# Tanh results in a four-buffer pool, three attention pairs begun a step earlier, weight sums begun later

## The chip, the core and the metric

The kernel runs on one NeuronCore of a Trainium2 chip. The metric is the device time of one execution in microseconds (us). Engines are named as in the profile: PE is TensorE's matmul, PEld its weight load, DVE is VectorE, ACT is ScalarE, POOL is GpSimd, and SP issues the transfers.

## The reference

Masked attention for 8 batches and 8 heads (576 rows, head size 64): the first four heads see a local band of 32 keys, the other four see every 32nd key. Its output, 4608 tokens of 512, goes through a two-layer network with a gate.

```python
scores = scale * np.matmul(q, k.transpose(0, 1, 3, 2))
scores = np.where(masks[None, :, :, :], scores, -1000000000.0)
scores = scores - np.max(scores, axis=-1, keepdims=True)
attn = np.exp(scores)
attn = attn / (np.sum(attn, axis=-1, keepdims=True) + 1e-09)
...
h = x @ w_in
g = h * (1.0 / (1.0 + np.exp(-1.702 * h)))
return (g @ w_out).astype(np.float32)
```

## The kernel before, in words

**Tiles and stages.** Tokens are cut into 9 groups of 512 (`NG`), the hidden width of 2048 into 16 blocks of 128 (`NF`). Each fp32 matrix is held as a high and a low part (`gh`, `gl`; `w_0` is the tile of both parts of an input weight block, `w_1` of an output weight block), and a product is three matmuls. The first three groups (`NN`) go through 48 **steps** `s`, one for each group and block: `ffn1(s)` makes `h` (12 matmuls), `act(s)` makes tanh on ACT and the gate on DVE, `split(s)`, at the following step, makes `gh` on ACT and `gl` on DVE, and `second` multiplies block s-2 into four output banks `o` (12 matmuls). The other six groups go in three doubles through a scheme with fewer products, which needs sums of weight blocks. That part begins at about 333 us and is not edited.

**Weights.** In the first 16 steps the weights are also unpacked. For each of two items a step, ACT shifts the raw words (`raw`), DVE joins them (`join`), ACT copies the high part (`high`), and DVE subtracts the low part (`low`). The weight block that is finished in step s is read by `ffn1(s+1)`.

**Attention in pairs.** Attention is done in pairs of head groups beside the steps. Pairs 0 to 4 come first. Pairs 5 to 9 are `apart`, the first group: they are turned in steps 5, 7, 9, 11 and 13 (`TURNS`). At step `begin[p]` a pair has its scores (PE: `s`), mask and maximum (DVE). Between `begin[p]` and `turn[p]` ACT makes its eight exponentials, spread over the steps between; what is left is run at step `turn[p]`, ahead of `high`. Then come a reciprocal (DVE), a multiply by it (POOL: `pr<-pr,rinv`), the transposes (DVE: `pt_s`, `pt_l`), and two steps after the turn the product with V (PE: `sa`), which ACT copies and DVE subtracts into `xs` or `xl`.

**Sums.** For each of 8 pairs of weight blocks `add_up(c)` runs six adds on POOL at the end of step `SUMS[c]`; two steps later ACT makes the high part (`plain<-summed`), three steps later DVE the low part, and SP stores eight pieces (`s<-plain`, `s<-summed`). The tiles come from one pool of 42 buffers shared with weights and attention results, so `summed` of block pair 1 takes the buffer that `plain` of block pair 0 left, and POOL waits until its stores have landed.

**Order.** Every engine keeps the order in which the program is written. No planner changes it; pools choose buffers. One pool of four buffers (`st2`) holds the output tiles of groups 0 and 1 until their stores have landed, one word tile, and, later, results of the doubles. The banks `c` of pairs 10 and later share six PSUM banks with `h` and `o`.

Of the kernel before, what the change touches and what calls it, by code (L numbers as in the profile page):

```python
# [9 lines left out]
F32 = mybir.dt.float32  # L10
# [8 lines left out]
P = 128  # L19
# [21 lines left out]
G = 512  # L41
# [12 lines left out]
AHEAD = 2  # L54
# [6 lines left out]
TURNS = ((5, 7, 9, 11, 13), (1, 3, 5, 7, 9, 11, 13, 15), (1, 3, 5, 7, 9, 11, 13))  # L61
BLOCKS = ("a11", "s2", "a12", "s3", "a22", "s1", "s4")
OPENING = ("a11", "a12", "s1", "s2", "s3", "a22", "s4")
SUMS = (17,19,21,29,31,33,35,37)
CUTS = (256, 384, 512)
PLAN = {
# [38 lines left out]
def attn_ffn(ctx, tc, lqk, sqk, lv, sv, w_in, w_out, masks, out):  # L105
# [7 lines left out]
    ffn = ctx.enter_context(tc.tile_pool(name="ffn", bufs=2))  # L113
# [7 lines left out]
    def st2(shape, dtype, name):  # L121
        return st.tile(shape, dtype, tag="st2", name=name, bufs=NT)
# [228 lines left out]
    apart = range(n0, n0 + len(windows[0]))  # L351
# [188 lines left out]
    g2s = {}  # L540

    def act(s):
        ps = hps.pop(s)
        g2 = g2s[s] = ffn.tile([P, G], F32, tag="g2", name=f"g2_{s}", bufs=1)
        scalar.activation(g2, ps, AF.Tanh, scale=0.851)
        vector.scalar_tensor_tensor(
            out=g2, in0=g2, scalar=1.0, in1=ps, op0=ALU.add, op1=ALU.mult
        )
# [137 lines left out]
    for p in (n0, n0 + 1):  # L686
        load_qk(p)
        load_v(p)
    act(0)
    weigh(3)  # L690
    split(0)
    begin_word(5)
    act(1)

    turn = {}
    p = n0
# [6 lines left out]
        turn[p + i] = len(steps) + 2 + 2 * i  # L703
    begin = {p: turn[p] - 3 for p in turn}
    for p in turn:
        if p - AHEAD in turn:
            begin[p] = turn[p - AHEAD] + (3 if p - AHEAD in apart else 2)

    sums = [
# [36 lines left out]
    def sum_up(s, end):  # L746
        for c in range(NF // 2):
            at = s - SUMS[c]
            if at == 0 and end:
# [234 lines left out]
    for s in range(2, len(steps)):  # L984
# [17 lines left out]
        for k in now:  # L1002
            low(k)
        act(s)
        ahead(s, False)
        sum_up(s, False)
# [28 lines left out]
    p = plain[-1] + 1  # L1035
# [8 lines left out]
    for d, (a, b) in enumerate(DOUBLES):  # L1044
# [20 lines left out]
        p = more.stop  # L1065
# [127 lines left out]
```

## Time and profile before

| | |
|---|---|
| median of 3 runs | 866.83 us (866.13 to 870.11) |
| profiled execution | 866.99 us, span 865.2 us, granted clock 0.99 |
| PE busy | 848.6 us, 98% |
| PEld busy | 689.6 us, 80% |
| DVE, ACT, POOL busy | 557.9, 439.6, 198.7 us |

Matmuls overlap in the profile, so that PE appears busy nearly always; how densely it is fed shows in PEld, the weight loads, one for each matmul. Every helper records its operations on one line of the source, L142, so tiles and not lines tell operations apart. Below, a step is named by when its `h` begins: step 9 at 77.71 us, step 10 at 85.67, step 15 at 126.09.

### The profile page before, as it was taken

How to read it: one execution, taken by the hardware profiler on the slowest of the kernel's cores; microseconds unless marked ns; L12 is line 12 of the kernel's file. 1: busy time of each engine (PE TensorE's matmuls, PEld its weight loads, DVE VectorE, ACT ScalarE, POOL GpSimd, SP SyncE). 2: the span in 40 equal slices, each digit the busy share in tenths (PEclk: the TensorE clock that was granted, in tenths of full speed). 3: DMA queues.
4: the chain of work that ended last, by engine and by line, in shares of the span. 5: the costliest groups of instructions: out<-in, count | busy, mean ns of one | idle time of the engine just before them, and what ended most of it. 6: DMA issues, size and time to landing. Idle time of an engine off the chain costs nothing.

```text
span 865.2 us, 17304 instructions
## 1 busy us (share of the span) xinstructions
PE 848.6 (98%) x6538; PEld 689.6 (80%) x6538; DVE 557.9 (64%) x989; ACT 439.6 (51%) x1330; POOL 198.7 (23%) x177
## 2 busy tenths in 40 slices
PE   8999989999999999999999999999999999999998
PEld 5887768877888888888888788888888888888886
DVE  4788977566587777766767776766766554444522
ACT  7798776453465555545545654545534433332321
POOL 4001003421366100423332011232230012232200
PEclk9899999999999999999999999999999999999999
DMA  9774324675165416666667645656655255454432
GB/s 341 298 283 152 121 62 145 203 229 175 47 225 167 153 47 207 195 204 214 182 192 233 191 135 162 219 172 196 182 165 177 72 164 166 151 169 142 149 119 74
DMA packets 76164, 148.87 MB, mean 172 GB/s; under 512 B 8240, under 2 KB 22960, under 8 KB 76080
## 3 DMA queue, kind: packets, MB, share of 16 engines
q1 hardware_dynamic: 76080, 147.76, 53.3%
q8 instruction: 52, 0.85, 0.4%
q14 instruction: 32, 0.26, 0.1%
HBM read 111.03 MB, written 36.70 MB: 171 GB/s over the span
## 4 chain that ended last, share of the span: by engine, by line
PE 88%; DVE 4%; ACT 3%; DMA 2%; SPq 1%; issue 1%; POOL 0%; ACTq 0%; DVEq 0%; POOLq 0%
PE o L142 42%; PE hs L142 15%; PE h L142 13%; PE ha L142 11%; PE sa L142 3%; PE c L142 2%; ACT pr L142 2%; SPq L142 1%; DMA s<-plain 1%; DVE w L142 1%; PE t L142 1%; DVE pt_l L142 1%; DMA a<-w 1%; PE s L142 1%; PE a L142 1%
## 5 line engine op out<-in xcount | busy, mean ns | idle before, releaser
L142 PE MATMUL o<-w,gh 128*128 128x512 f32 x1152 | 379.7, 391 | 0.1
L142 PEld LDWEIGHTS o<-w,gh 128*128 128x128 f32 x1152 | 216.5, 188 | 44.8 <-ACT out L142 0.6
L142 PE MATMUL o<-w,gl 128*128 128x512 f32 x576 | 228.3, 396 | 0.0
L142 POOL TENSOR_TENSOR gl<-y,gh 128x512 fp32r<-128x512 f32 x45 | 61.7, 1372 | 293.1 <-PE ha L142 149.8
L142 PEld LDWEIGHTS o<-w,gl 128*128 128x128 f32 x576 | 108.3, 188 | 24.3 <-DVE gl L142 0.2
L142 POOL TENSOR_TENSOR pr<-pr,rinv 128x432 f32<-128x432 f32 (+1 forms) x42 | 48.9, 1164 | 244.1 <-DVE rinv L142 244.1
L142 DVE SCALAR_TENSOR_TENSOR y<-tanh,y 128x512 f32<-128x512 f32 x96 | 67.8, 707 | 55.6 <-ACT tanh L142 55.5
L142 ACT ACTIVATE pr<-pr,nmax 128x54 f32<-128x54 f32 (+1 forms) x296 | 101.0, 344 | 4.9 <-DVE nmax L142 4.9
L142 ACT ACTIVATE tanh<-y 128x512 f32<-128x512 f32 x96 | 60.7, 632 | 67.5 <-DVE y L142 66.9
L142 PE MATMUL h<-xl,w 128*128 128x512 f32 x288 | 77.0, 403 | 5.6 <-ACT w L142 3.3
L142 PE MATMUL h<-xs,w 128*128 128x512 f32 x288 | 75.2, 397 | 0.0
L142 DVE TENSOR_TENSOR spare<-hs,spare 128x512 f32<-128x512 f32 x69 | 47.7, 691 | 38.9 <-PE hs L142 38.9
L142 DVE TENSOR_TENSOR gl<-spare,gh 128x512 fp32r<-128x512 f32 x48 | 33.2, 691 | 56.3 <-ACT gh L142 56.1
L142 PEld LDWEIGHTS h<-xl,w 128*128 128x128 f32 x288 | 54.0, 192 | 18.8 <-ACT w L142 3.7
L142 PEld LDWEIGHTS h<-xs,w 128*128 128x128 f32 x288 | 55.5, 193 | 11.9
L142 ACT CAST gh<-spare 128x512 fp32r<-128x512 f32 x48 | 29.9, 623 | 63.8 <-PE o L142 62.4
L142 DVE STREAM_TRANSPOSE pt_l<-pr 32x256 f32<-32x256 f32 x128 | 55.7, 435 | 5.8 <-POOL pr L142 3.7
L142 ACT ACTIVATE g<-h 128x512 f32<-128x512 f32 x48 | 28.7, 597 | 60.4 <-DVE gl L142 32.8
L142 DVE STREAM_TRANSPOSE pt_s<-pr 32x256 f32<-32x256 f32 x126 | 54.8, 435 | 3.1 <-POOL pr L142 1.1
L142 ACT ACTIVATION_READ_ACCUMULATOR pr<-pr,nmax 128x1 f32 x296 | 55.7, 188 | 0.0
L142 DVE SCALAR_TENSOR_TENSOR g<-g,h 128x512 f32<-128x512 f32 x48 | 32.9, 685 | 30.8 <-ACT g L142 30.8
L142 ACT COPY spare<-ha 128x512 f32<-128x512 f32 x24 | 14.1, 586 | 72.3 <-PE ha L142 72.3
(131 smaller groups left out, 1249.5 us busy)
## 6 DMA issues: line engine op xcount, KB each, us to landing
stream<-s SPq DMA_DIRECT2D x96, 256.0 KB, 2.7
stream<-a SPq DMA_DIRECT2D x72, 256.0 KB, 2.8
gate<-y SPq DMA_DIRECT2D x48, 256.0 KB, 2.6
spare<-gate SPq DMA_DIRECT2D x48, 256.0 KB, 2.8
qk<-sqk SPq DMA_DIRECT2D x23, 452.0 KB, 3.5
qk<-lqk SPq DMA_DIRECT2D x18, 576.0 KB, 3.9
v<-lv SPq DMA_DIRECT2D x18, 512.0 KB, 5.5
out<-out SPq DMA_DIRECT2D x36, 256.0 KB, 2.8
```

The lines of the kernel that those rows point to most:

```text
L142: ins = call(*args, **kw)
```

## The change

Three edits. The tanh of the 48 steps writes into a tile of the four-buffer pool `st2` and no longer into a single buffer `g2`. Pairs 7, 8 and 9 begin three steps ahead of their turn (at 6, 8 and 10) and no longer one step ahead (8, 10 and 12). The sums of block pair 1 move from step 19 to step 21, those of block pair 2 from 21 to 29, and each later one moves two steps, the last from 37 to 39.

```diff
-SUMS = (17,19,21,29,31,33,35,37)
+SUMS = (17, 21, 29, 31, 33, 35, 37, 39)
...
     def act(s):
         ps = hps.pop(s)
-        g2 = g2s[s] = ffn.tile([P, G], F32, tag="g2", name=f"g2_{s}", bufs=1)
+        g2 = g2s[s] = st2([P, G], F32, f"g2_{s}")
         scalar.activation(g2, ps, AF.Tanh, scale=0.851)
...
     for p in turn:
-        if p - AHEAD in turn:
+        if p - AHEAD in turn and p not in apart:
             begin[p] = turn[p - AHEAD] + (3 if p - AHEAD in apart else 2)
```

On ACT, from the end of step 8 into step 9, the order differs as follows. `gh` is the high part of the gate, `pr_98` the exponentials of pair 7, `w_0` and `w_1` the high parts of the weights of which the next `h` reads the first, `g_9` the tanh.

```order
-L142 CAST gh_1124<-g_8_1062 128x512
-L142 ACTIVATE pr_98,ssum_1128<-pr_98,nmax_1105 128x54 x8
-L142 ACTIVATE rinv_1137<-ssum_1128 128x8
-L142 CAST w_0_1141<-raw_860 128x512
-L142 CAST w_1_1143<-raw_863 128x512
-L142 ACTIVATE g_9_1151<-h_1109 128x512
+L142 ACTIVATE pr_98,ssum_1015<-pr_98,nmax_967 128x54 x4
+L142 CAST gh_1157<-g_8_1091 128x512
+L142 ACTIVATE rinv_1161<-ssum_1015 128x8
+L142 CAST w_0_1165<-raw_860 128x512
+L142 CAST w_1_1167<-raw_863 128x512
+L142 ACTIVATE g_9_1175<-h_1142 128x512
```

Eight exponentials stood between `gh` and the weights' high parts; now the last four stand ahead of `gh`, at the end of step 8, and nothing long stands ahead of the weights. The first four have moved to the end of step 7, where ACT's order in the changed kernel is this (`xs_0` are the copies of pair 5's product with V):

```order
L142 ACTIVATE raw_783<-raw_783 128x512 x2
L142 ACTIVATE pr_98,ssum_1015<-pr_98,nmax_967 128x54 x4
L142 CAST xs_0_311<-sa_5_1032 128x2x14x6
L142 CAST xs_0_311<-sa_5_1033 128x2x14x6
L142 CAST xs_0_1050<-sa_5_1032 128x2x4x6
L142 CAST xs_0_1050<-sa_5_1033 128x2x4x6
L142 CAST gh_1077<-g_7_1004 128x512
```

The copies that stood right behind `raw` now come four exponentials later. Steps 9 to 13 change in the same way for pairs 8 and 9.

On POOL, before, from the end of step 19 (`plain`, `summed` are tiles of the sums, `pr_97` and `pr_98` the scaled exponentials of pairs 12 and 13):

```order
L142 TENSOR_TENSOR plain_1961<-w_0_514 128x512
L142 TENSOR_TENSOR plain_1961<-w_0_646 128x512
L142 TENSOR_TENSOR summed_1962<-plain_1961 128x256 x2
L142 TENSOR_TENSOR summed_1962<-summed_1962,plain_1961 128x256
L142 TENSOR_TENSOR summed_1962<-plain_1961,summed_1962 128x256
L142 TENSOR_TENSOR pr_97<-pr_97,rinv_2045 128x8x54
L142 TENSOR_TENSOR plain_2118<-w_0_722 128x512
L142 TENSOR_TENSOR plain_2118<-w_0_775 128x512
L142 TENSOR_TENSOR summed_2119<-plain_2118 128x256 x2
```

In the changed kernel the same place reads:

```order
L142 TENSOR_TENSOR pr_97<-pr_97,rinv_2037 128x8x54
L142 TENSOR_TENSOR plain_2109<-w_0_514 128x512
L142 TENSOR_TENSOR plain_2109<-w_0_646 128x512
L142 TENSOR_TENSOR summed_2110<-plain_2109 128x256 x2
L142 TENSOR_TENSOR summed_2110<-summed_2110,plain_2109 128x256
L142 TENSOR_TENSOR summed_2110<-plain_2109,summed_2110 128x256
L142 TENSOR_TENSOR pr_98<-pr_98,rinv_2184 128x768
L142 TENSOR_TENSOR pr_97<-pr_97,rinv_2335 128x768
```

The multiply of pair 12 now precedes the sums of block pair 1, and the multiply of pair 13 no longer has the sums of block pair 2 ahead of it.

## Rows read from the trace of the kernel before

**Rows 1.** The page: busy time, share of the span and instructions of each engine.

```profile
PE   848.6 (98%) x6538; PEld 689.6 (80%) x6538; DVE 557.9 (64%) x989; ACT 439.6 (51%) x1330; POOL 198.7 (23%) x177
```

**Rows 2.** Busy time by stretches of 40 us; last three: PEclk, DMA share, GB/s.

```profile
80.00:120.00 40.00, 34.43 (x340) 26.23 (x339) 33.00 (x63) 29.92 (x93) 3.29 (x3) 0.94 0.37 120
...
160.00:200.00 40.00, 36.77 (x356) 29.62 (x355) 26.52 (x50) 18.67 (x75) 12.00 (x13) 0.96 0.76 243
...
240.00:280.00 40.00, 40.00 (x409) 32.64 (x408) 31.34 (x54) 22.44 (x79) 25.65 (x26) 1.00 0.61 193
```

**Rows 3.** Same view: steps 3 to 8, then steps 9 to 14.

```profile
42.30:77.71 35.41, 35.41 (x247) 28.62 (x241) 32.27 (x59) 33.16 (x88) 2.91 (x2) 1.00 0.59 216
...
77.71:126.09 48.38, 42.81 (x406) 32.83 (x400) 40.59 (x77) 36.52 (x107) 3.29 (x3) 0.93 0.33 106
```

**Rows 4.** PE in order of time: start, us, what, [idle before and its releaser].

```profile
85.67 0.73 PE L142 MATMUL h<-xl,w 128*128 128x512 f32 x2 [1.16 <-ACT w L142]
...
102.94 1.20 PE L142 MATMUL h<-xl,w 128*128 128x512 f32 x4 [1.11 <-DVE w L142]
...
117.72 0.80 PE L142 MATMUL h<-xl,w 128*128 128x512 f32 x2 [2.14 <-ACT w L142]
```

**Rows 5.** The chain that ended last, at step 9.

```profile
82.14 2.71 ACT pr L142 x16
```

**Rows 6.** Waits of DVE, 65.8 to 129.3 us: total us, times, longest.

```profile
DVE rinv L142 <- ACT rinv L142: 4.1, 3, 1.5
DVE w L142 <- ACT w L142: 3.2, 6, 0.7
```

**Rows 7.** DVE in order of time: the pairs of low parts of weights.

```profile
69.64 2.52 DVE L142 TENSOR_TENSOR w<-raw,w 128x512 fp32r<-128x512 f32 x2
...
85.65 1.87 DVE L142 TENSOR_TENSOR w<-raw,w 128x512 fp32r<-128x512 f32 x2 [0.33 <-ACT w L142]
...
91.87 1.28 DVE L142 TENSOR_TENSOR w<-raw,w 128x512 fp32r<-128x512 f32 x2
...
101.08 2.41 DVE L142 TENSOR_TENSOR w<-raw,w 128x512 fp32r<-128x512 f32 x2 [0.35 <-ACT w L142]
```

**Rows 8.** POOL in order of time, steps 21 to 24.

```profile
167.48 1.43 POOL L142 TENSOR_TENSOR summed<-plain 128x256 f32<-128x256 f32 x2 [12.81 <-DMA s<-plain]
...
170.38 0.91 POOL L142 TENSOR_TENSOR pr<-pr,rinv 128x432 f32<-128x432 f32 x1
171.25 2.54 POOL L142 TENSOR_TENSOR plain<-w 128x512 f32<-128x512 f32 x2
183.16 1.43 POOL L142 TENSOR_TENSOR summed<-plain 128x256 f32<-128x256 f32 x2 [9.37 <-DMA s<-plain]
...
186.06 1.47 POOL L142 TENSOR_TENSOR pr<-pr,rinv 128x768 f32<-128x768 f32 x1
```

**Rows 9.** PE in order of time: step 23 begins; a wait in step 25.

```profile
174.37 1.52 PE L142 MATMUL h<-xl,w 128*128 128x512 f32 x6
...
196.65 1.06 PE L142 MATMUL c<-qk 64*64 64x54 f32 x30 [1.21 <-DVE g L142]
```

**Rows 10.** The chain that ended last: first `h` of steps 27, 31, 33, 39 and 41.

```profile
205.46 2.72 PE h L142 x12
...
230.30 2.72 PE h L142 x12
...
242.73 2.72 PE h L142 x12
...
281.24 2.72 PE h L142 x12
...
293.89 2.72 PE h L142 x12
```

**Rows 11.** Issues, KB each, median us to landing: stores of group 0, then group 1.

```profile
out<-out SPq DMA_DIRECT2D x4, 256.0 KB, 2.4
...
out<-out SPq DMA_DIRECT2D x2, 256.0 KB, 3.3
```

## The prediction

> **What bounds the kernel now.** The page comes first: PE is busy for 98% of the span, but its weight loads fill only 80% [rows 1]. So I read PEld as the measure of how densely PE is fed, and the busy time by stretches of 40 us shows where it is not. At 240 to 280 us, where the steps run smoothly, loads take 32.64 of 40 us; at 80 to 120 us they take 26.23, at 160 to 200 us 29.62, and there the mean granted clock is 0.94 and 0.96 and not 1.00 [rows 2]. These two places are the kernel's losses ahead of the doubles, and the edits touch both. Everywhere else PE sets the pace, and work moved on other engines costs nothing while it stays covered.
>
> The first place is steps 9 to 14, 48.38 us. DVE works 40.59 of them and ACT 36.52, while in steps 3 to 8 DVE works 32.27 of 35.41 and PEld 28.62 [rows 3]. So DVE is nearly full before and not full in the stalled steps, though it is what PE waits for. PE's own rows tell why: it stands at the first matmuls of `h` in steps 10, 12 and 14, for the high parts of the weights (ACT) or the low ones (DVE) [rows 4]. The chain runs at step 9 through sixteen ACT pieces, the eight exponentials of pair 7 with their accumulator reads, 2.71 us [rows 5], which stand ahead of the high parts. DVE waits for what ends this burst: 4.1 us in three places for the reciprocal's input [rows 6].
>
> The second place is steps 21 to 26. POOL stands 12.81 and then 9.37 us at the first add into `summed`, until stores of the sums before have landed, and the multiplies of pairs 12 and 13 (170.38 and 186.06 us) stand behind these sums [rows 8]. Their transposes, and so the product with V, come late.
>
> **The pairs.** No operation is added: eight exponentials, two mask operations and a maximum for each of three pairs move two steps forward, and with them the scores on PE and one transfer of the next pair on SP's queue. The exponentials leave the place ahead of the high parts. DVE gets back the 4.1 us of waiting for `rinv` [rows 6] and three waits of 0.33 to 0.35 us for the high part right behind it, of which two are shown [rows 7]: about 1.0 us. Against this stand two prices. Without that last wait the low parts follow the reciprocal at once, as now in step 7, where the pair took 2.52 us; in steps 9 and 11 it took 1.87 and 2.41 us, beside 1.28 without a multiply on POOL [rows 7]. That is 0.1 us for each of three, 0.3 in all. And four exponentials, half of 2.71 us [rows 5], now stand ahead of ACT's copies of the product with V, for which DVE waits next. This happens at three copies, so it costs from nothing to 4.1 us. DVE mostly arrives later than they do, since the moved mask is now ahead of it, and I take 0.7, half of one such delay. DVE gains 4.1 + 1.0 - 0.3 - 0.7 = **4.1 us**, and since DVE's work is the scarce thing there, so does the time. The bounds are nothing (the new waits eat all) and all idle time of DVE in these steps, 48.38 - 40.59 = 7.8 us [rows 3]. By PEld the upper bound is the same: at the density of steps 3 to 8 (28.62 of 35.41) its 32.83 us would fill 40.6 us, which leaves 7.8. The extra mask work in steps 6 and 8 falls where DVE is already 91% full [rows 3]. I price it at nothing, because PE has the moved scores in the same steps; without this cover it would be part of the 0.7.
>
> The rows say that a multiply of 0.91 or 1.47 us [rows 8] adds 0.6 or 1.1 us to the pair of low parts [rows 7]. The Trainium skill ("SBUF — State Buffer", section "Who interferes with whom") states a harder rule: a VectorE operation with two SBUF inputs and a GpSimd operation that reads SBUF shut each other out for a whole instruction. By that rule alone each of the three multiplies would take its full length from DVE, 3.3 us together where the rows give 2.3 to 2.6, and the gain of the pairs would be some 0.7 us less, 3.4.
>
> **The sums.** Block pair 1's sums now start two steps later. The multiply of pair 12 no longer stands behind a wait, and the six adds behind it meet stores that are landed or nearly so: the wait that ended at 167.48 us ended with the last of them, and the two `plain` adds ahead of the first `summed` take 2.54 us [rows 8]. The sums of block pair 2 leave this stretch. So steps 23 to 26 should take what steps of the same content take later. From the first `h` of step 23 (174.37 us) [rows 9] to that of step 27 (205.46) is 31.09 us. Steps 31 and 32 hold the same products as 23 and 24 and take 242.73 - 230.30 = 12.43 us; steps 39 and 40 match 25 and 26 and take 293.89 - 281.24 = 12.65 us [rows 10]. The difference is 31.09 - 25.08 = **6.0 us**. The bounds are 4.5, if a quarter of it comes from something else than POOL, and 6.3. The sums that now fall in steps 29 to 37 lie where they do now; the last set, in step 39, lies on POOL, ACT and DVE in a stretch like 240 to 280 us, where five sets cost PE nothing: DVE is busy 31.34 of 40 us there and the clock is 1.00 [rows 2].
>
> **The tanh.** Tanh no longer waits for the low part of the step before. Where DVE paces, that low part is done before ACT gets there, so I give it nothing. Where it mattered, in step 25, PE waited 1.21 us for `g` at the bank of new scores [rows 9]; this is already in the 6.0. The new cost: in steps 17 and 33 the four output tiles share the four buffers with tanh tiles, so the fourth output waits until the first store has landed. Behind it on ACT stand `gh` and the next tanh, for which DVE and then PE wait. A store lands 2.4 us (group 0) or 3.3 us (group 1) after its issue [rows 11]. `gh` is read by PE two steps after its own, so a whole step, some 6.3 us (25.08 / 4), covers that: nothing, with a bound of 1 us.
>
> **Sum.** 4.1 + 6.0 + 0 = 10.1 us against the profiled execution's own 866.99 us (span 865.2 and 1.8 around it; 0.16 above the median of the runs): **856.9 us**. What a measurement of this kernel can tell from no change is about 0.5%, 4.3 us.
>
> **The rivals.**
> 1. *The pairs give nothing*: DVE is simply full, and ACT's later copies become its new wait. For it: 91% in the steps before [rows 3]. Against it: its named waits for the burst, 4.1 us [rows 6], are real idle time. Time: 866.99 - 6.0 = 861.0.
> 2. *All of the loss comes back*: 866.99 - 7.8 - 6.0 = 853.2. For it: three steps like these ran at full density beside pairs 5 and 6, begun three steps ahead. Against it: those steps started with DVE less behind.
> 3. *The sums do not come back*: the adds of block pair 1 still wait on stores, since the margin of 167.48 against the new start is small, and hold the multiply of pair 13. Time: 866.99 - 4.1 = 862.9. Against it: two steps lie between, and nothing of block pair 2 follows.
> 4. *Slower*: the output tile that waits in the tanh pool holds ACT so long that PE starves in steps 17 and 33. To end 4.3 us above 866.99 it must eat the 10.1 too, 14.4 us or 7.2 at each place, behind a cover of about 6.3: a landing of over 13 us. The stores take 2.4 and 3.3 [rows 11]. If it did happen: 871.3 or more.
>
> **How the numbers follow.** Forecast (855 to 859.5) 0.63, rival 1 0.14, rival 2 0.13, rival 3 0.06, rival 4 0.02, no change at all 0.02. Faster by over 0.5% means under 862.5: the forecast, rivals 1 and 2 and a third of rival 3, 0.92; the rest of rival 3 and no change, 0.06 within; 0.02 slower. The range from 852.5 to 861.5 takes in the forecast and most of rivals 1 and 2.
>
> **What would show it.** In the profile after, steps 9 to 14 take about 44 us, PE's waits at the weights shrink below 1 us each, and the mean clock from 80 to 120 us nears 1.00; DVE's wait for `rinv` is gone. POOL's two waits for stores are gone or under 2 us, and four steps from step 23 take about 25 us. The fourth output's evacuation in steps 17 and 33 starts later, with no wait of PE behind it. I am wrong if DVE's idle time in steps 6 to 14 stays near 8 us under other names, if POOL waits again at `summed`, or if PE loses time in steps 39 to 42.

## The result and the profile after

The changed kernel takes **856.01 us** (median of 4 runs, 855.29 to 858.87) against 867.16 us of the kernel before beside it (4 runs): ratio 0.9872, 95% interval 0.9838 to 0.9906. Its profiled execution took 855.29 us, 11.70 less than that of before.

The page's busy line, and the view of busy time by stretch (length, then PE, PEld, DVE, ACT, POOL, then granted clock, DMA share, GB/s), for steps 3 to 8, steps 9 to 14, and the two stretches of [rows 2]:

```profile
PE 842.1 (99%) x6538; PEld 683.9 (80%) x6538; DVE 554.9 (65%) x989; ACT 439.5 (51%) x1330; POOL 199.8 (23%) x177
```

```profile
42.57:79.02 36.45, 36.45 (x279) 29.25 (x273) 33.57 (x62) 34.66 (x96) 2.90 (x2) 1.00 0.61 223
79.02:119.75 40.73, 39.04 (x373) 29.97 (x369) 37.42 (x73) 34.29 (x97) 4.12 (x3) 1.00 0.34 115
...
80.00:120.00 40.00, 38.31 (x366) 29.39 (x366) 36.73 (x72) 33.31 (x95) 4.12 (x3) 1.00 0.35 117
160.00:200.00 40.00, 40.00 (x453) 32.60 (x453) 26.31 (x54) 18.70 (x75) 9.04 (x9) 1.00 0.73 229
```

From 80 to 120 us weight loads rose from 26.23 to 29.39 us and the clock from 0.94 to 1.00; from 160 to 200 us loads rose from 29.62 to 32.60, the density of smooth steps. Steps 9 to 14 take 40.73 us in place of 48.38, and DVE is idle in 3.31 of them (40.73 - 37.42), no longer in 7.8.

The timeline of PE in steps 9 to 15, only the rows in which it waited (start, length, and in brackets the idle time and what ended it), answers to [rows 4]:

```profile
93.42 1.19 PE L142 MATMUL h<-xl,w 128*128 128x512 f32 x4 [0.36 <-DVE w L142]
106.17 0.73 PE L142 MATMUL h<-xl,w 128*128 128x512 f32 x2 [0.99 <-ACT w L142]
107.20 1.19 PE L142 MATMUL h<-xl,w 128*128 128x512 f32 x4 [0.29 <-DVE w L142]
120.65 1.19 PE L142 MATMUL h<-xl,w 128*128 128x512 f32 x4 [0.17 <-DVE w L142]
127.41 0.50 PE L142 MATMUL o<-w,gh 128*128 128x512 f32 x1 [0.22 <-DVE w L142]
```

No wait exceeds 1 us; before, the longest was 2.14. POOL's timeline, which answers to [rows 8], shows no wait at `summed`:

```profile
158.93 0.91 POOL L142 TENSOR_TENSOR pr<-pr,rinv 128x432 f32<-128x432 f32 x1 [11.99 <-DVE rinv L142]
159.79 2.53 POOL L142 TENSOR_TENSOR plain<-w 128x512 f32<-128x512 f32 x2
162.46 1.43 POOL L142 TENSOR_TENSOR summed<-plain 128x256 f32<-128x256 f32 x2
...
171.50 1.47 POOL L142 TENSOR_TENSOR pr<-pr,rinv 128x768 f32<-128x768 f32 x1 [6.11 <-DVE rinv L142]
```

To see where time went in this and every run, I took the first weight load of each step's `h` in each profile and the time between them, in us:

```
steps               3-8    9-15   16-22  23-26  27-32  33    34-46   3-46
before              35.41  57.38  39.06  30.93  37.27  7.25  80.93   288.23
changed kernel      36.45  50.83  39.06  25.09  37.27  6.95  81.01   276.66
pairs only          36.45  50.86  39.06  31.55  37.27  7.27  80.95   283.42
sums only           35.41  57.41  39.06  25.09  37.27  7.29  81.75   283.28
tanh only           35.41  58.80  39.06  26.61  37.27  6.95  80.96   285.07
without the tanh    36.45  50.82  39.06  25.09  37.27  7.26  81.73   277.68
```

Steps 3 to 15 gave 5.5 us (92.79 to 87.28), steps 23 to 26 gave 5.84, step 33 gave 0.30, steps 34 to 46 lost 0.08: 11.57 of the 11.70. Of the 1.04 us that steps 3 to 8 are longer, 0.93 is one set of scores that now stands in step 6 (5.44 before, 6.37 after).

### The profile page after: what moved, and what is told of

Its sections match the earlier page's. It is cut to its first block, busy times and chain, and to the rows that moved or that the text cites. A ratio compares the mean times of both kernels' runs of the same rounds, so it can differ in the third digit from the quotient of the medians.

```text
span 853.5 us, 17279 instructions
## 1 busy us (share of the span) xinstructions
PE 842.1 (99%) x6538; PEld 683.9 (80%) x6538; DVE 554.9 (65%) x989; ACT 439.5 (51%) x1330; POOL 199.8 (23%) x177
## 4 chain that ended last, share of the span: by engine, by line
PE 89%; DVE 6%; ACT 3%; DMA 1%; issue 1%; SPq 0%; DVEq 0%; ACTq 0%
PE o L142 43%; PE hs L142 15%; PE h L142 12%; PE ha L142 11%; PE sa L142 3%; PE c L142 2%; DVE raw L142 1%; DVE w L142 1%; ACT raw L142 1%; PE t L142 1%; ACT pr L142 1%; DVE pt_l L142 1%; DVE pt_s L142 1%; DMA raw<-w_out 1%; DVE gl L142 1%
## 5 line engine op out<-in xcount | busy, mean ns | idle before, releaser
L142 PE MATMUL h<-xs,w 128*128 128x512 f32 x288 | 73.4, 390 | 0.0
L142 DVE SCALAR_TENSOR_TENSOR pr<-c,masks_sb 128x216 f32<-128x216 f32 (+1 forms) x60 | 25.0, 458 | 39.7 <-PE c L142 39.6
```

The costliest lines, as they stand in the source:

```text
L142: ins = call(*args, **kw)
```

## The experiments

Each ran beside the kernel before; a ratio is to those runs. Ratios that overlap are not told apart by the times; there the table's stretches decide, which repeat within some 0.2 us between profiles wherever a run leaves the stretch as it was, except where the text says otherwise.

**1. The pairs alone.**

```diff
-        if p - AHEAD in turn:
+        if p - AHEAD in turn and p not in apart:
```

> Of the three edits only the early start of pairs 7, 8 and 9. My theory: the time comes from the eight exponentials leaving the place ahead of the weights' high parts, so this edit alone gives what the changed kernel shows there: step 9 to step 15 in about 41 us (48.4 before), step 15 one us longer than before, 5 to 6 us in all, about 861.5 us; steps 23 to 26 stay at about 31 us. Rival: the tanh in a pool of four is part of that gain, since ACT no longer stands at the tanh for the low part of the gate; then the pairs alone bring only the 4.1 us of the prediction or less, and step 9 to step 15 takes 44 us or more.

Measured: 862.41 us, ratio 0.9945 (0.9926 to 0.9964). Steps 3 to 15 take 87.31 us as in the changed kernel; in this one profile steps 23 to 26 are 0.6 longer than before, at a mean clock of 0.89 and not 0.94. The pairs give their 5.5 us without the other edits. (They begin two steps earlier than before, at 6, 8 and 10, and not one step, as the title has it.)

**2. The sums alone.**

```diff
-SUMS = (17,19,21,29,31,33,35,37)
+SUMS = (17, 21, 29, 31, 33, 35, 37, 39)
```

> Of the three edits only the later sums. My theory: steps 23 to 26 take about 25.2 us (31 before), nothing else moves by more than 0.5 us, about 861 us. Rival: part of that gain is the tanh's, which no longer waits for the low part of the gate; then steps 23 to 26 keep 1 us or more of the loss.

Measured: 863.21 us, 0.9950 (0.9935 to 0.9965). Steps 23 to 26 take 25.09 us, so the tanh isn't needed there. But step 43 takes 7.53 us against 6.74 before: ACT's timeline in this run shows the tanh of that step standing for the low part of the gate, long after the high part,

```profile
301.65 0.61 ACT L142 CAST gh<-g 128x512 fp32r<-128x512 f32 x1
...
305.61 0.60 ACT L142 ACTIVATE g<-h 128x512 f32<-128x512 f32 x1 [3.24 <-DVE gl L142]
```

and in DVE's timeline that low part stands behind three subtractions of 1.2 us, the last of them the low part of the moved sums, and behind transposes:

```profile
302.20 1.22 DVE L142 TENSOR_TENSOR summed<-summed,plain 128x1024 fp32r<-128x1024 f32 x1
...
304.82 0.69 DVE L142 TENSOR_TENSOR gl<-g,gh 128x512 fp32r<-128x512 f32 x1
```

In the changed kernel `gl` stands behind the same work, but the tanh of that step waits for PE alone:

```profile
297.95 0.60 ACT L142 ACTIVATE g<-h 128x512 f32<-128x512 f32 x1 [1.64 <-PE h L142]
```

**3 and 4. Two ways by which late sums could reach PE**, each taken away from the kernel before: the multiplies of pairs 12 and 13 on DVE, and the high and low parts of block pair 2 one step later.

```diff
-        gpsimd.tensor_tensor(
+        engine = vector if p in (12, 13) else gpsimd
+        engine.tensor_tensor(
             out=pr[:, :, :nk],
```

> The kernel before, with the multiplies of pairs 12 and 13 on DVE and the sums at their old steps. My theory as in the prediction: the loss in steps 23 to 26 comes by the multiply that stands behind POOL's wait for stores, so with the multiply elsewhere 4 to 5 of the 6 us return although POOL still waits some 12 and 9 us: steps 23 to 26 in 26 to 27 us, about 862.5 us. Rival: ACT's wait of 5.8 us for the sums, with the high part of the gate and the next tanh behind it, makes the loss alone; then steps 23 to 26 still take 30 us or more and the time stays within 1 us of before, or is longer by the two multiplies on DVE.

Measured: 863.25 us, 0.9952 (0.9934 to 0.9970). Steps 23 to 26 take 28.93 us: 2.0 of 6 us came back, neither theory. The medians fell by 4.2 us (interval 2.6 to 5.7); the profiled execution, 865.37 us, is one of the two slowest of seven, so what the others gained beyond the 2.0 stands in no profile. PE's wait for `pt_l` fell from 1.3 to 0.3 us; of its two waits for the gate, 2.0 us in all, the longer stayed, in the view of waits from step 23 to 26:

```profile
PE c L142 <- DVE g L142: 1.2, 1, 1.2
PE sa L142 <- DVE pt_l L142: 0.3, 1, 0.3
```

In DVE's timeline `gl` now waits for `gh`, which stands on ACT behind 5.4 us of waiting for the late sums:

```profile
188.21 0.69 DVE L142 TENSOR_TENSOR gl<-g,gh 128x512 fp32r<-128x512 f32 x1 [2.59 <-ACT gh L142]
```

```diff
-            if at == 2 and end:
+            late = 1 if c == 2 else 0
+            if at == 2 + late and end:
                 high_sums(c)
-            if at == 3 and not end:
+            if at == 3 + late and not end:
```

> The kernel before, with the high and low parts of the sums of block pair 2 one step later (steps 24 and 25 in place of 23 and 24); its adds stay at step 21, and the multiplies stay behind them on POOL. My theory: the multiply of pair 13 is as late as before, so steps 23 to 26 still take 29 us or more. Rival: ACT's wait of 5.8 us for these sums makes the loss; then it is gone, steps 23 to 26 take 27 us or less, and the time falls by 4 us or more.

Measured: 868.79 us, 1.0022 (1.0008 to 1.0035), a little longer than before. Steps 23 to 26 take 31.51 us: as my theory had it, this alone returns nothing. ACT's wait for the sums is gone in these steps, but ACT's timeline shows the next tanh standing for `gl`, which DVE makes behind transposes that wait 3.7 us for the late multiply:

```profile
191.15 0.60 ACT L142 ACTIVATE g<-h 128x512 f32<-128x512 f32 x1 [7.17 <-DVE gl L142]
```

**5. Both ways away.**

> The kernel before, with both edits of the two runs ahead: multiplies of pairs 12 and 13 on DVE, and high and low parts of the sums of block pair 2 one step later. Alone, the first brought steps 23 to 26 from 30.9 to 28.9 us and the second left them at 31.5. My theory now: POOL's late sums reach PE by two ways side by side, the late multiply and ACT's wait for the sums, so the second edit pays once the first is made: steps 23 to 26 in 25.1 to 26.5 us, POOL still waiting some 22 us, about 861.5 us. Rival: the second edit gives nothing here either, since the two multiplies on DVE or later waits hold PE: 28 us or more, about 863.5 us.

Measured: 865.52 us, 0.9981 (0.9965 to 0.9998). Steps 23 to 26 take 25.93 us, as expected, while POOL still waits 22 us for its buffers. But step 27 takes 9.26 us in place of 7.20: the later parts mean later stores, and DVE now stands for one of them before it may write an attention result into a buffer of the same pool.

```profile
DVE xl L142 <- DMA s<-plain: 3.2, 1, 3.2
```

That is part of why the time fell by only 1.3 us and not by some 5. So the loss had two ways side by side, and POOL's own waiting costs little there (25.93 us against 25.09). The two ways meet at `gl`. The timelines of DVE and ACT of the kernel before show it where step 25 begins:

```profile
187.57 1.78 DVE L142 STREAM_TRANSPOSE pt_l<-pr 32x256 f32<-32x256 f32 x4 [3.66 <-POOL pr L142]
189.38 0.69 DVE L142 TENSOR_TENSOR gl<-g,gh 128x512 fp32r<-128x512 f32 x1
...
190.17 0.60 ACT L142 ACTIVATE g<-h 128x512 f32<-128x512 f32 x1 [2.46 <-DVE gl L142]
```

`gh`, late by ACT's wait for the sums, is done at 187.71 us, the transposes that had waited for the multiply at 189.35; `gl` stands behind both, and the next tanh behind `gl`.

**6. The burst kept.** The changed kernel with all eight exponentials of pairs 7 to 9 at the turn.

```diff
-            if begin[p] < s < t:
+            if begin[p] < s < t and p not in (7, 8, 9):
```

> The changed kernel, in which pairs 7, 8 and 9 have their scores, mask and maximum three steps ahead, but all eight exponentials in the step of the turn, ahead of the high parts, as before. My theory: the burst on ACT is the cause, so the gain of the pairs is lost: steps 9 to 15 take 56 to 58 us (50.8 in the changed kernel, 57.4 before), DVE waits for the reciprocal's input again, about 861.5 us. Rival: the gain comes from the mask and the scores leaving the crowded steps; then steps 9 to 15 stay below 53 us, and the time below 858.

Measured: 857.48 us, 0.9896 (0.9878 to 0.9914). Steps 3 to 15 take 89.06 us. With the burst in its old place 3.7 of the 5.5 us remain: my theory falls. Its rival named the work that leaves; but the waits of ACT in the kernel before show something else, which I had not read:

```profile
ACT w L142 <- DVE raw L142: 7.9, 5, 2.6
ACT pr L142 <- DVE nmax L142: 4.9, 3, 1.9
ACT w L142 <- DVE w L142: 3.5, 3, 1.3
```

ACT stood 4.9 us for the maxima of the very pairs whose exponentials came next. DVE's and ACT's timelines of the kernel before at the first of these places, the end of step 8, show why:

```profile
78.92 1.79 DVE L142 STREAM_TRANSPOSE pt_l<-pr 32x256 f32<-32x256 f32 x4
80.74 0.67 DVE L142 SCALAR_TENSOR_TENSOR pr<-s,masks_sb 128x216 f32<-128x216 f32 x2
81.44 0.60 DVE L142 TENSOR_REDUCE nmax<-pr 128x8 f32<-128x432 f32 x1
```

```profile
82.14 0.34 ACT L142 ACTIVATE pr<-pr,nmax 128x54 f32<-128x54 f32 x1 [1.64 <-DVE nmax L142]
```

The mask stands behind 1.79 us of transposes, so the burst starts 1.64 us late, and with it the reciprocal's input and the high parts. In the run with the burst kept ACT's wait at `nmax` is gone and DVE's wait for the reciprocal's input falls from 4.1 to 1.0 us, although the burst is as long as before.

**7. The mask first.** The kernel before, with the transposes moved behind the mask and maximum in steps 8, 10 and 12 (and, by the same lines, in step 14, where pair 10 begins; ACT had no wait for its maximum).

```diff
-            if t + 1 == s:
-                run(turning[p], 2)
         behind = second(*steps[s - LAG], s - LAG) if s >= LAG and s != NF else iter(())
...
         visit([p for p in turn if turn[p] + 2 == s], [p for p in turn if begin[p] == s])
+        for p, t in turn.items():
+            if t + 1 == s:
+                run(turning[p], 2)
```

> The kernel before with one change of DVE's order: in steps 8, 10 and 12 the mask and maximum of pairs 7, 8 and 9 come ahead of the transposes of the pair before them, and not behind (1.3 to 1.8 us of transposes). No work changes its step, and the eight exponentials stay ahead of the high parts. The run with the burst kept showed that my first theory (the burst's place) fails. My theory now: before, ACT stood 4.9 us in three places for these maxima, and everything behind the burst came late by that; with the maxima earlier that wait falls below 1 us, and steps 3 to 15, 92.8 us before, take 89 to 90.5 us: 2 to 4 us less, about 864 us. Rival: in the changed kernel it counts that scores and mask leave the crowded steps 9 to 14; here none leaves, so steps 3 to 15 stay at 92.3 us or more, the time within 0.7 us of before.

Measured: 862.07 us, 0.9950 (0.9926 to 0.9974). Steps 3 to 15 take 88.66 us: 4.1 us come from an exchange of neighbours on one engine. In the timelines of DVE and ACT of this run the maximum ends before ACT has finished `gh`, and the exponentials follow with no wait:

```profile
78.33 0.67 DVE L142 SCALAR_TENSOR_TENSOR pr<-s,masks_sb 128x216 f32<-128x216 f32 x2
79.03 0.60 DVE L142 TENSOR_REDUCE nmax<-pr 128x8 f32<-128x432 f32 x1
79.67 1.81 DVE L142 STREAM_TRANSPOSE pt_l<-pr 32x256 f32<-32x256 f32 x4
```

```profile
79.45 0.60 ACT L142 CAST gh<-g 128x512 fp32r<-128x512 f32 x1
79.96 0.34 ACT L142 ACTIVATE pr<-pr,nmax 128x54 f32<-128x54 f32 x1
```

ACT's wait for maxima is 0.4 us in all, DVE's for the reciprocal's input is gone. That work leaves the crowded steps isn't needed for this part.

**8. The tanh back in one buffer**, the other edits kept.

```diff
-        g2 = g2s[s] = st2([P, G], F32, f"g2_{s}")
+        g2 = g2s[s] = ffn.tile([P, G], F32, tag="g2", name=f"g2_{s}", bufs=1)
```

> The changed kernel with the tanh back in a single buffer. The run with the sums alone lost 0.8 us at step 43 that the changed kernel does not lose, beside ACT waits of 7.7 us at tanh for the low part of the gate. My theory now: the tanh edit is worth what stands there and 0.3 us in step 33, about 1.1 us in all, 857.1 us, with steps 3 to 32 as in the changed kernel. Rival: the prediction's nothing: within 0.4 us of the changed kernel, step 43 at 6.8 us.

Measured: 856.42 us, 0.9886 (0.9871 to 0.9900): not told apart from the changed kernel by the time. In the profile steps 3 to 46 take 1.02 us more, 0.31 at step 33 and 0.75 at step 43, and nothing elsewhere.

**9. Block pair 1 back at step 19.**

```diff
-SUMS = (17, 21, 29, 31, 33, 35, 37, 39)
+SUMS = (17, 19, 29, 31, 33, 35, 37, 39)
```

> The changed kernel with the sums of block pair 1 back at step 19; those of block pair 2 and the later ones stay moved. My theory: POOL's first wait for stores, some 12.7 us, is back and with it the late multiply of pair 12, so steps 23 and 24 lose about the 1.1 us that they lost before; the second wait stays gone, and steps 25 and 26 lose nothing: steps 23 to 26 in about 26.2 us, about 857.1 us. Rival: the first wait alone is covered; steps 23 to 26 stay at 25.1 us.

Measured: 855.39 us, 0.9871 (0.9856 to 0.9886). Steps 23 to 26 take 25.09 us although POOL waits 13 us and the multiply of pair 12 stands behind it again:

```profile
162.57 1.43 POOL L142 TENSOR_TENSOR summed<-plain 128x256 f32<-128x256 f32 x2 [12.99 <-DMA s<-plain]
...
165.47 0.92 POOL L142 TENSOR_TENSOR pr<-pr,rinv 128x432 f32<-128x432 f32 x1
```

My theory is wrong here: that wait is covered, and the first of the two moves that the prediction spoke of gives nothing in this kernel. What the sums gain beside the tanh edit comes from block pair 2 and the sets behind it. But the tanh edit is part of this run, and with the tanh alone (experiment 10) step 23 takes 6.95 us, as here, in place of 8.07 before; no run shows what this move gives with the single buffer.

**10. The tanh alone.**

> Of the three edits only the tanh in the pool of four. With the other two edits in place its removal cost 1.0 us in the profile: 0.3 in step 33 and 0.75 in step 43, where a set of sums now stands three steps ahead. My theory: the second part is owed to the moved sums, so alone the edit brings the 0.3 us of step 33 and at most 1.2 us of PE's wait for the gate in step 25, nothing in steps 3 to 15: 0.3 to 1.5 us, about 866 us. Rival: with ACT free of that wait more of steps 23 to 26 returns, 2 us or more, about 864 us.

Measured: 863.57 us, 0.9945 (0.9924 to 0.9966). Steps 23 to 26 take 26.61 us: 4.3 of the 5.8 us come back with the sums where they were. The rival is right. In ACT's timeline of this run ACT waits for the late sums as before, but the next tanh follows `gh` at once and no longer waits for `gl`, as it did for 2.46 us in the kernel before:

```profile
188.38 1.05 ACT L142 CAST plain<-summed 128x1024 fp32r<-128x1024 f32 x1 [4.54 <-POOL summed L142]
189.34 0.61 ACT L142 CAST gh<-g 128x512 fp32r<-128x512 f32 x1
189.86 0.59 ACT L142 ACTIVATE g<-h 128x512 f32<-128x512 f32 x1
```

Steps 9 to 15 took 58.80 us in this profile, 1.4 longer than before, at a mean clock of 0.91 and not 0.94, with the same waits of PE (5.4 us). The difference stands in step 14: 10.01 us at a mean clock of 0.66, before 8.37 at 0.80. Nothing in the edit accounts for a clock that stays low for longer, and its cause stays open.

**11 and 12. Two tries at the rest**, both on the changed kernel: the low parts of the gate on POOL in steps 4 to 14, and the reciprocals of pairs 7 to 9 ahead of the joins.

```diff
-        vector.tensor_tensor(out=gl, in0=g2, in1=gh.bitcast(F32), op=ALU.subtract)
+        engine = gpsimd if 4 <= s < 15 else vector
+        engine.tensor_tensor(out=gl, in0=g2, in1=gh.bitcast(F32), op=ALU.subtract)
```

> The changed kernel with the low parts of the gate of steps 4 to 14 on POOL in place of DVE (11 operations, 0.68 us each on DVE). My theory: DVE is what remains short from step 9 to 15 (50.8 of 55 us busy from 70 to 125 us); it loses 7.5 us of work there, steps 9 to 15 take 48 to 49.5 us in place of 50.8, about 854.5 us. Rival: operations on POOL hold up DVE's, as the low parts beside a multiply did; each then costs DVE what it saves, or PE waits for the slower POOL: 50.8 us or more, 856 us or above.

Measured: 862.93 us, 0.9949 (0.9929 to 0.9969); steps 9 to 15 take 54.60 us, and steps 3 to 8 2.0 us more than in the changed kernel. Groups of DVE and POOL from the start of step 4 to that of step 16 (count, then busy time and mean ns of one), first in this run, then in the changed kernel:

```profile
L142 DVE SCALAR_TENSOR_TENSOR raw<-raw 128x512 uint32<-128x512 uint32 x23 | 21.4, 965 | 0.5 <-ACT raw L142 0.4
L142 DVE TENSOR_TENSOR w<-raw,w 128x512 fp32r<-128x512 f32 x23 | 21.0, 931 | 4.7 <-ACT w L142 4.4
...
L142 POOL TENSOR_TENSOR gl<-g,gh 128x512 fp32r<-128x512 f32 x11 | 16.1, 1466 | 79.4 <-ACT gh L142 79.4
```

```profile
L142 DVE TENSOR_TENSOR w<-raw,w 128x512 fp32r<-128x512 f32 x23 | 18.9, 849 | 2.3 <-ACT w L142 2.2
L142 DVE SCALAR_TENSOR_TENSOR raw<-raw 128x512 uint32<-128x512 uint32 x23 | 14.9, 685 | 0.5 <-ACT raw L142 0.4
...
L142 DVE TENSOR_TENSOR gl<-g,gh 128x512 fp32r<-128x512 f32 x12 | 8.2, 685 | 1.2 <-ACT gh L142 1.1
```

DVE lost 11 low parts, 7.5 us of work, and got 8.6 back in joins and low parts of the weights that run beside POOL (21.4 - 14.9 + 21.0 - 18.9). The rival holds.

```diff
+        for p in (7, 8, 9):
+            if turn.get(p) == s:
+                run(soft.pop(p))
         for k in now:
             join_word(k)
...
-            if t == s:
+            if t == s and p not in (7, 8, 9):
                 run(soft.pop(p))
```

> The changed kernel with the reciprocal of pairs 7, 8 and 9 ahead of DVE's join of the raw words in the step of the turn, so that POOL's multiply (1.2 to 1.75 us) no longer runs beside the two low parts of the weights (2.52 us in place of 1.29 beside the longest multiply). My theory: the multiply holds up the joins there as much as the low parts, as POOL's low parts of the gate did in the run ahead (joins 1.02 us in place of 0.69), so the delay only changes its place: steps 9 to 15 between 50.3 and 51.3 us, the time within 0.6 us of the changed kernel. Rival: the low parts are what POOL's multiply delays most; then up to 2.4 us return, steps 9 to 15 in 49 us or less, about 854 us.

Measured: 858.87 us, 0.9893 (0.9868 to 0.9918); steps 9 to 15 take 54.21 us, 3.4 more. The delay changed its place as I said, here at pair 8:

```profile
98.02 2.52 DVE L142 SCALAR_TENSOR_TENSOR raw<-raw 128x512 uint32<-128x512 uint32 x2
101.06 1.28 DVE L142 TENSOR_TENSOR w<-raw,w 128x512 fp32r<-128x512 f32 x2
```

The join took 2.52 us and the low part 1.28, the exchange of what the changed kernel shows (1.28 and 2.52). But the place matters, and both theories missed that: ACT's high parts wait for the joins (9.8 us, 8.4 in the changed kernel), so a late join delays two engines where a late low part delays one. DVE also waits 1.1 us for the reciprocal's input, which it did not in the changed kernel, and 1.8 us more for the copies of the product with V; no run separates these.

No run told a kernel apart from the changed one as faster. The one with block pair 1 left at step 19 has the same time.

## Why the prediction was right, and where its working failed

**What bounds.** The two places were the right ones: 11.3 of the 11.7 us come from steps 3 to 15 and 23 to 26. Of the signs named ahead, PE's waits below 1 us, the clock at 1.00, DVE's wait for `rinv` gone, POOL's waits gone and four steps from step 23 in about 25 us (25.09) all came; steps 9 to 14 took 40.73 us where I said about 44, and step 15 gave 1.1 back.

**The pairs, 4.1 us: measured 5.5.** The size is within the bounds, but the cause that the prediction put ahead, that the exponentials leave the place ahead of the high parts, is the smaller part. With the burst kept, 3.7 us remain; spreading it adds 1.8. The larger part is that ACT waited 4.9 us for maxima that DVE made late, behind transposes; exchanging the two alone gives 4.1. The 4.1 us of DVE waiting for `rinv` were the echo of this, one engine further, so the sum came out near for a reason that I had not seen, by luck as much as by working. In the view of [rows 5] the two pieces right ahead of the burst are the mask and the maximum:

```profile
80.74 0.68 DVE pr L142 x2
81.44 0.61 DVE nmax L142
```

The step that was missing was to ask what the burst itself had waited for, and what stood ahead of that on DVE.

**The clock** was not in the sum. Before, the mean granted clock was 0.81 in step 10 and 0.80 in step 14, so part of each ran at 1.2 and not at 2.4 GHz; ahead of both PE had stood, 1.16 and 2.14 us at the start of these steps [rows 4]. Over steps 9 to 15 it was 0.94 before and is 1.00 after, which could be up to 3.4 us (0.06 x 57.38). PE's waits for weights in this stretch fell by 3.5 us (5.5 to 2.0). But the two do not add up, and the clock set little of the time here. With the multiplies of pairs 12 and 13 on DVE (experiment 3), an edit that does not touch these steps, the clock was 0.97, PE waited 6.4 us in place of 5.5, and the stretch took the same time (the kernel before, then this run):

```profile
77.71:135.09 57.38, 51.81 (x474) 40.00 (x469) 47.69 (x93) 42.90 (x127) 3.29 (x3) 0.94 0.35 112
78.56:135.94 57.38, 51.05 (x474) 38.96 (x468) 47.70 (x93) 42.94 (x127) 3.29 (x3) 0.97 0.34 112
```

Where the clock fell less, PE waited longer for the weights; only at 0.91, with the tanh alone, did these steps take longer. In steps 23 to 26 the clock has a share that the runs do not separate: it was 0.94 before and with the multiplies on DVE, and 1.00 with the tanh alone, with both ways away and in the changed kernel. My estimate is up to 1.9 us (0.06 x 30.93), beside 3.3 us of PE's waits that are gone.

**The small prices** held: DVE's waits for the copies of the product with V rose from 1.5 to 2.1 us (0.7 taken), its waits for high parts of weights fell from 3.4 to 2.8 us (1.0 taken), and the moved masks and scores cost nothing beyond the 0.93 us of scores that steps 9 to 14 lose.

**The sums, 6.0 us: measured 5.84.** The comparison with later steps of the same content gave the size; the mechanism was half wrong. The multiplies behind POOL's wait are there, but taken away alone they return 2.0 us in the profile (experiment 3), because a second way runs through ACT: the high part of the late sums holds `gh`, and `gh` holds `gl`. By either way `gl` was late and held the next tanh in its single buffer, and PE stood for the gate at the bank of new scores; with only that last link taken away 4.3 us return (experiment 10). And the move of block pair 1, of which the prediction said the most, gives nothing beside the tanh edit (experiment 9).

**The tanh, nothing: 1.0 to 4.6 us, by what stands beside it.** That step failed. The prediction took the wait of step 25 for something that the sums' move takes away, which is right, but not for something that the tanh takes away as well. The two edits cover the same 4.3 us, either of them enough; with the sums moved, the tanh is left with 0.3 us in step 33 and 0.75 in step 43. That last part corrects another step: the set of sums moved to step 39 was said to cost nothing, and without the tanh edit it costs 0.8 us. The price feared for the tanh came and was covered: ACT waits 1.7 us in step 17 and 2.5 in step 33 for an output store, with no wait of PE behind it. The 3.3 us of [rows 11] were read from two of group 1's four stores; all four took 3.2 to 6.0 us to land, still less than the cover.

The rivals: the pairs gave nothing (no), all of the loss returns (853.2: in steps 9 to 14 nearly, 7.65 of 7.8, but 1.0 us went in steps 3 to 8 and 1.1 in step 15), the sums do not come back (no), slower (no).

## What to carry to other kernels

When a burst on one engine heads the chain, look first at what it waited for: an exchange of two neighbours on the engine that feeds it may give most of what moving the burst gives. Where two edits remove links of one chain, each can be worth most of it alone and next to nothing beside the other, so price each with the other made and not made. And an engine that waits 13 us may cost nothing at all; only the instruction behind it that someone else waits for says whether it does.

## What the runs showed of the hardware

Work moved from DVE to an idle POOL came back as longer DVE operations: 11 low parts, on the mean 1.47 us each on POOL, added 8.6 us to DVE's joins and low parts of the weights, 0.78 us each, where each takes 0.68 us on DVE itself.

In the run with the early reciprocals one multiply of POOL, begun 0.23 us after a pair of joins, stretched that pair from 1.28 to 1.96 us and took 1.18 us itself; a longer one stretched the pair to 2.52 us and took 1.74. The same multiplies take 0.91 and 1.47 us where DVE has nothing of this kind beside them [rows 8], and also in the kernel before, where they begin 0.2 us ahead of the low parts, whose pair then took 1.87 and 2.41 us [rows 7]. POOL's timelines show the two multiplies of the kernel before, then the longer one of the run with the early reciprocals:

```profile
85.46 0.91 POOL L142 TENSOR_TENSOR pr<-pr,rinv 128x432 f32<-128x432 f32 x1 [13.84 <-DVE rinv L142]
100.87 1.47 POOL L142 TENSOR_TENSOR pr<-pr,rinv 128x768 f32<-128x768 f32 x1 [14.49 <-DVE rinv L142]
```

```profile
98.25 1.74 POOL L142 TENSOR_TENSOR pr<-pr,rinv 128x768 f32<-128x768 f32 x1 [13.10 <-DVE rinv L142]
```

So a multiply that began first kept its length, one that began second took 0.27 us more, and DVE's pair lost 0.23 to 0.34 us less than 0.91 or 1.47. The Trainium skill ("SBUF — State Buffer", section "Who interferes with whom") says that a DVE operation with two SBUF inputs and a GpSimd operation that reads SBUF contend for ports that work as an exclusive lock; the trace agrees to within that third of a microsecond. The same section of the Trainium skill says that a DVE operation with at most one SBUF input, outside what it calls the 2-port perf modes, does not contend; the trace agrees for DVE's transposes, of which three at 139.20 us in the changed kernel, beside POOL's adds, took 1.31 us, 0.44 each, as they do elsewhere (0.435).
